# A new order of all steps, with the state products of batches 2 to 7 in blocks of three slices

## The chip, the cores and the metric

The kernel runs on one core of a Trainium2 chip. The metric is the time of one execution on the device in microseconds (us), as a median of several runs. The engines are PE (matrix products; PEld is its loading of weights), DVE, ACT and POOL (elementwise work), and SP, which here only issues transfers. Each engine works through its own queue in order, and waits on semaphores for the others. Sixteen DMA engines move data; they are fed by the queues of SP, ACT and POOL.

## The reference

Two stages in a row. The first lets 512 tokens and 32 state rows per batch and head attend to each other; the second is a feed-forward layer with the snake function.

```python
B, H, S, Ns, D = (8, 8, 512, 32, 64)      # x: (B,H,S,D), state: (B,H,Ns,D)
a = softmax(scale * x @ state.T)          # over the 32 state rows
xread = a @ state
a2 = softmax(scale * state @ x.T)         # over the 512 tokens
sread = a2 @ x
attn = concatenate([xread, sread], axis=2)            # (B, H, 544, D)
x2 = attn.transpose(0, 2, 1, 3).reshape(8 * 544, 512)
h = x2 @ w_in                             # 512 -> 2048
s = sin(alpha * h)
g = h + s * s / (alpha + 1e-9)
out = g @ w_out                           # 2048 -> 512, float32
```

Both softmaxes come from one table of exponentials, since the scores of the second are the transposed scores of the first.

## The kernel before

The whole program is one list of steps in a text, `ORDER` (line 21 on). A step such as `sq.0.2.V` calls the method `sq` of the class `Steps` with (0, 2, "V"). The order of the text is the order in each engine's queue; steps of different engines overlap as the semaphores allow. A last letter A, V or G gives the engine (ACT, DVE, POOL); a number where a bank is meant is one of the eight PSUM banks (`k.ps`, line 194). Each bank is a pool with one buffer: a new tile in a bank waits until every reader of the tile before it is done.

The unit of the work is a batch b (0 to 7) of 512 tokens; t = 8 is the group of all 256 state rows.

- **Loads.** POOL issues, with conversion to bf16, `l_st` (state, line 265), `lx` (x of batches 1 to 7, line 271), `li` (w_in in four quarters, line 280) and `lo` (w_out in four quarters, line 292). SP issues `l_s01` (state of batches 0 and 1) and `lq` (x of batch 0). `xnat` has three buffers.
- **Attention of a batch.** `pk` (DVE, line 344) sorts the tokens into `xp`, `td` (SP, line 387) transposes xp by DMA into `xT`; for batch 1 it is done on PE with `xt` (line 371) and copies `xc`, for batch 0 with `xtq`. `sc` (line 394) makes the scores on PE, `ex` the exponentials on ACT (which needs another table than Sin; a change of table is an ACT_TABLE_LOAD), `rs` and `rr` the sums and reciprocals on DVE, `nm` (line 418) the normalized table A, `ad` (SP, line 438) its transpose AT by DMA; in batch 0 `at` and `ac` do that on PE. `w` and `cs` (lines 445, 456) make the state side, `rc` and `xs` finish it on DVE.
- **State products.** Instead of xread @ w_in the kernel multiplies the state with w_in: `m` (line 478) makes one or two slices of M = state @ w_in of a batch, 512 columns of the 2048 each, on tiles of 64 rows by 32 columns; a slice is 8 matmuls and fills two banks (g = 0, 1). `me` (line 495) copies each bank to `M` in bf16. Slice s serves the feature blocks f = 4s to 4s+3. `st_t` and `st_c` transpose the state of batches 2 to 7 first, `s01_t` and `s01_k` that of batches 0 and 1.
- **Feed-forward.** For each f of 16: `h` (two matmuls of M with AT, line 531; `hg` is one of the two, line 549), `si` (Sin on ACT), `sq` (square on ACT, DVE or POOL, line 564), `gt` (s2 / alpha + h on DVE, line 573), which gives gT, the weights of the last product. For each quarter st of a batch, `o` (line 581) adds 16 matmuls gT x w_out in one bank; `oc` copies the bank to `o_sb` (six buffers), `os` (SP, line 597) writes it out. For t = 8, `h` has four matmuls of 256 columns. The last tile of all, (7, 3), is made in two pieces of 384 and 128 columns: `oh`, `och`, `osh`.
- **Warm-up.** `warm_up.n.cols.bank` (line 300) are matmuls without use in the first 17 us.

In the text before, `m` of batches 2 to 7 is called twelve times for two slices (four banks) each; `o.t.st.f0.f1` runs f0 to f1 in a row and every tile goes through f in rising order; `M` has two buffers, so the products of batch b + 2 can start only when the last `h` of batch b is done.

## Time and profile before

| | |
|---|---|
| time, median of 3 runs | 221.43 us (221.27 to 221.89) |
| the profiled execution | 221.22 us |
| its span, first to last instruction | 219.2 us |
| granted TensorE clock | 1.00 |
| ACT Sin, x144 | 88.8 us busy, mean 670 ns |
| DVE gt, x144 | 96.8 us busy, mean 713 ns |
| squares on POOL x75, ACT x53, DVE x16 | mean 1022, 594, 439 ns |
| copies of M: ACT x35, DVE x29 | mean 594, 679 ns |
| table loads for Exp and Sin on ACT | 5 and 5, 1283 ns each |
| transposes by DMA, issue to landing | AT 3.3 us, xT 4.8 us (medians) |
| output of one o tile (256 KB), issue to landing | 2.3 us (median) |

The busy time of an engine is the time in which it ran instructions. Matmuls are pipelined: the mean duration of one (373 to 379 ns for 512 columns) is longer than the distance from one to the next, which is read from a group of them in the chain of waits. An entry "A <- B: total, times, longest" of the waits says that A stood idle until B was done. Windows and timelines are in us from the start of the span.

### The profile page before, as it was taken

What the parts mean: (1) busy time and instruction counts of PE and PEld (TensorE: products, weight loads), DVE (VectorE), ACT (ScalarE), POOL (GpSimd) and SP (SyncE); (2) the same over time, 40 slices, a digit from 0 to 9 for tenths busy, and PEclk for the clock granted to TensorE, in tenths of its full rate; (3) what the DMA queues carried; (4) which work ended last, traced back from release to release, by engine and by line L of the source; (5) the groups of instructions that cost most, each with busy time, mean ns of one, the idle gap of its engine ahead of it and who ended that gap; (6) DMA issues with size and microseconds to landing.
All of it is one profiled execution on the core that took longest, in us unless ns stands there. A gap on an engine that the chain in (4) does not pass through costs nothing.

```text
span 219.2 us, 4303 instructions
## 1 busy us (share of the span) xinstructions
PE 211.4 (96%) x1593; PEld 104.5 (48%) x1619; DVE 162.9 (74%) x287; ACT 173.4 (79%) x297; POOL 106.2 (48%) x114
## 2 busy tenths in 40 slices
PE   7989999999999999999999999999999999999994
PEld 3744544444444534444454444454445555665452
DVE  3769996999787789989888788888667987661201
ACT  4799778997998979898996999798848896785111
POOL 5959533895195647753943387273501082121000
PEclk9999999999999999999999999999999999999999
DMA  6999999987491029167145327470220211012042
GB/s 195 178 206 204 205 204 146 217 169 133 101 238 48 3 92 143 57 144 96 48 79 131 109 71 96 134 110 0 48 100 0 98 48 48 0 51 96 1 143 96
DMA packets 38052, 23.48 MB, mean 107 GB/s; under 512 B 20992, under 2 KB 33680, under 8 KB 38032
## 3 DMA queue, kind: packets, MB, share of 16 engines
q1 hardware_dynamic: 26128, 15.08, 26.5%
q0 software_dynamic: 11648, 8.13, 26.0%
q8 instruction: 12, 0.20, 0.3%
q14 instruction: 8, 0.07, 0.1%
q10 hardware_dynamic: 256, 0.01, 0.1%
HBM read 17.44 MB, written 8.91 MB: 120 GB/s over the span
## 4 chain that ended last, share of the span: by engine, by line
PE 90%; DMA 6%; POOL 1%; issue 1%; ACT 0%
PE o_ps L587 54%; PE h_ps L537 22%; DMA w_in_sb<-in_moe_w_in_dram 5%; PE m_ps L488 4%; PE h_ps L543 3%; PE h_ps L552 2%; PE w_ps L450 2%; PE s_ps L399 2%; PE w_ps L461 1%; DMA s<-in_state_dram 1%; POOL w_in_sb L282 1%; PE x_ps L376 0%; POOL st_nat L267 0%; POOL s01b L255 0%; ACT o_sb L595 0%
## 5 line engine op out<-in xcount | busy, mean ns | idle before, releaser
L587 PE MATMUL o_ps<-w_out_sb,gT 128*128 128x512 bf16 (+2 forms) x542 | 133.9, 373 | 1.6 <-issue 1.0
L576 DVE SCALAR_TENSOR_TENSOR gT<-s,inva_sb,h_ps 128x512 bf16<-128x512 bf16 (+1 forms) x144 | 96.8, 713 | 20.4 <-POOL s L201 10.8
L201 POOL TENSOR_TENSOR s<-s 128x512 bf16<-128x512 bf16 (+1 forms) x75 | 75.9, 1022 | 64.4 <-ACT s L560 62.7
L560 ACT ACTIVATE s<-h_ps,alpha_sb 128x512 bf16<-128x512 f32 (+1 forms) x144 | 88.8, 670 | 11.1 <-PE h_ps L543 4.5
L587 PEld LDWEIGHTS <-gT 128*128 128x128 bf16 x560 | 52.3, 98 | 60.3 <-issue 5.0
L537 PE MATMUL h_ps<-AT,M 128*128 128x512 bf16 x219 | 60.0, 379 | 0.3
L537 PEld LDWEIGHTS <-M 128*128 128x128 bf16 x224 | 21.7, 98 | 25.9 <-issue 0.4
L569 ACT ACTIVATE s<-s 128x512 bf16<-128x512 bf16 (+1 forms) x53 | 31.4, 594 | 0.8
L201 POOL TENSOR_TENSOR A<-E,rR 128x512 bf16<-128x512 bf16 x16 | 16.6, 1056 | 23.8 <-ACT o_sb L595 12.9
L595 ACT COPY o_sb<-o_ps 128x512 f32<-128x512 f32 (+2 forms) x24 | 13.7, 570 | 16.6 <-PE o_ps L587 16.5
L496 ACT CAST M<-m_ps 128x512 bf16<-128x512 f32 x35 | 18.6, 594 | 8.2 <-PE m_ps L488 8.2
L496 DVE CAST M<-m_ps 128x512 bf16<-128x512 f32 x29 | 18.9, 679 | 2.5 <-PE m_ps L488 2.1
L595 DVE COPY o_sb<-o_ps 128x512 f32<-128x512 f32 x11 | 7.5, 685 | 12.9 <-PE o_ps L587 12.9
L201 DVE TENSOR_TENSOR s<-s 128x512 bf16<-128x512 bf16 (+1 forms) x16 | 7.0, 439 | 6.2 <-ACT s L560 6.1
L410 DVE TENSOR_REDUCE R<-E 128x16 f32<-128x512 bf16 x16 | 10.4, 657 | 0.7 <-ACT E L406 0.6
L488 PE MATMUL m_ps<-w_in_sb,stT 64*32 64x512 bf16 x256 | 10.2, 382 | 0.1
L468 DVE RECIPROCAL rC<-w_ps 128x128 f32<-128x128 f32 x8 | 7.6, 948 | 3.3 <-PE w_ps L461 3.2
L303 PE MATMUL warm_ps<-warm 128*128 128x128 bf16 (+3 forms) x66 | 8.6, 271 | 1.4 <-DVE warm L209 1.2
L552 PE MATMUL h_ps<-AT,M 128*128 128x512 bf16 x29 | 8.4, 379 | 0.9 <-ACT M L496 0.7
L406 ACT ACTIVATE E<-s_ps 128x512 bf16<-128x512 f32 x16 | 8.8, 602 | 0.4 <-PE s_ps L399 0.4
L543 PE MATMUL h_ps<-xs_all,w_in_sb 128*128 128x256 bf16 x64 | 9.1, 273 | 0.0
L543 PEld LDWEIGHTS <-w_in_sb 128*128 128x128 bf16 x64 | 6.3, 98 | 3.4
(56 smaller groups left out, 101.8 us busy)
## 6 DMA issues: line engine op xcount, KB each, us to landing
out_dram<-o_sb SPq DMA_DIRECT2D x33, 256.0 KB, 2.3
xnat<-in_x_dram POOLq DMA_DIRECT2D x7, 512.0 KB, 7.5
w_in_sb<-in_moe_w_in_dram POOLq DMA_DIRECT2D x4, 512.0 KB, 10.9
w_out_sb<-in_moe_w_out_dram POOLq DMA_DIRECT2D x4, 512.0 KB, 18.0
x<-in_x_dram SPq DMA_DIRECT2D x4, 256.0 KB, 4.2
st_nat<-in_state_dram POOLq DMA_DIRECT2D x1, 256.0 KB, 5.3
out_dram<-o_sb SPq DMA_DIRECT2D x1, 192.0 KB, 1.9
s<-in_state_dram SPq DMA_DIRECT2D x1, 128.0 KB, 2.2
```

Source lines behind the costliest of these rows:

```text
L201: {"V": k.nc.vector, "G": k.nc.gpsimd}[eng].tensor_tensor(out, a, b, ALU.mult)
L410: k.nc.vector.reduce_sum(R[:, g], k.t["E", b][:, g].rearrange("p c (h j) -> p (c h) j", j=k.Ns), axis=AX.X)
L488: k.nc.tensor.matmul(k.t["m", b, s + n, g][o0:o0 + k.Ns, :], k.stT[k.half(r), b * k.G + g, c0:c0 + k.Ns], k.w_in_sb[k.half(r), 2 * g + h, ...
L496: k.copy(eng)(k.t["M", b][:, g, s * k.FW:(s + 1) * k.FW], k.t["m", b, s, g][:])
L537: k.nc.tensor.matmul(hp[:, :n], k.t["M", t][:, g, fs], k.t["AT", t][:, g, :], start=(g == 0), stop=(g == k.G - 1),)
L543: k.nc.tensor.matmul(hp[:, :n], k.w_in_sb[:, q, fs], k.xs_all[:, q].rearrange("p b j -> p (b j)"), start=(q == 0), stop=(q == k.Q - 1),)
L552: k.nc.tensor.matmul(k.t["h", t, f][:], k.t["M", t][:, g, f * k.P:(f + 1) * k.P], k.t["AT", t][:, g, :], start=(g == 0), stop=(g == k.G - 1),)
L560: k.nc.scalar.activation(s[:, :n], k.t["h", t, f][:, :n], ACT.Sin, scale=k.alpha_sb[:, f:f + 1])
L569: k.nc.scalar.activation(s2[:, :n], s[:, :n], ACT.Square)
L576: k.nc.vector.scalar_tensor_tensor(gT[:, :n], k.t["s2", t, f][:, :n], k.inva_sb[:, f:f + 1], k.t["h", t, f][:, :n], ALU.mult, ALU.add,)
L587: k.nc.tensor.matmul(k.t["o", t, st, half][:, cols], k.t["gT", t, f][:, rows], k.w_out_sb[:, f, cols], start=(f == 0), stop=(f == k.FT - 1),)
L595: k.copy(eng)(o_sb[:, cols], k.t["o", t, st, half][:, cols])
```

## The change

The list of steps is replaced as a whole. Each step still does what it did, with these differences in the functions: `M` gets a third buffer; `xt` transposes both heads of a pair at once from `xp` (it read `xnat` one head at a time), so that it now stands behind `pk`; `hg` may take its two halves, and `o` its 16 feature blocks, in any order, with the bank taken by steps of their own (`ho`, `oo`) and the first and last matmul found by counting (`made`).

```diff
-        k.mpool, k.epool, k.smallp = pool("mpool", 2), pool("epool", 4), pool("smallp", 4)
+        k.mpool, k.epool, k.smallp = pool("mpool", 3), pool("epool", 4), pool("smallp", 4)
...
-                for r in range(2):
-                    k.nc.tensor.transpose(
-                        tp[k.half(r), h, i * k.P:(i + 1) * k.P],
-                        k.t["xnat", b][:, 2 * (2 * g + h) + r, i * k.D:(i + 1) * k.D],
-                        k.ident[:],
-                    )
+                k.nc.tensor.transpose(
+                    tp[:, h, i * k.P:(i + 1) * k.P], k.pair(b, i, 2 * g + h), k.ident[:]
+                )
...
+    def ho(k, t, f, bank):
+        k.t["h", t, f] = k.ps(bank, [k.P, k.S], FP32, "h_ps")
+        k.made["h", t, f] = 0
...
-            start=(g == 0), stop=(g == k.G - 1),
+            start=k.made["h", t, f] == 1, stop=k.made["h", t, f] == k.G,
...
+    def oo(k, t, st, bank, half=None):
+        k.t["o", t, st, half] = k.ps(bank, [k.P, k.DOUT], FP32, "o_ps")
+        k.made["o", t, st, half] = 0
+
+    def o(k, t, st, f, half=None):
...
+        k.made["o", t, st, half] += 1
+        k.nc.tensor.matmul(
+            k.t["o", t, st, half][:, cols], k.t["gT", t, f][:, rows], k.w_out_sb[:, f, cols],
+            start=k.made["o", t, st, half] == 1, stop=k.made["o", t, st, half] == k.FT,
+        )
```

Of the list, the parts of which the prediction speaks. The head:

```diff
-zero.1 identf.V lq.3.S s01_c.G l_st li.0 xq.0.A s01_t.4 li.1 xtq.0.5 warm_up.1.384.3 xq.1.A
-s01_k.1.V s01_k.0.A li.2 xtq.1.6 warm_up.2.448.3 xc.0.0.0.V xq.2.A xc.0.0.1.V lo.0 al_t.7 xq.3.A
...
+touch_x l_s01 consts touch lq.0.S ident_ l_alpha lq.1.S zero.0 warm_up.8.512.7 exp_table lq.2.S
+zero.1 identf.V lq.3.S s01_c.G li.0 xq.1.A warm_up.1.256.7 s01_t.0 warm_up.1.512.7 xtq.1.1 xq.0.A
+xtq.0.2 xq.2.V xtq.2.3 s01_k.0.A xq.3.V xtq.3.4 xc.0.0.1.A li.1 xc.0.0.0.A s01_k.1.V sc.0.0.0 ex.0.0
+xc.0.1.1.V xc.0.1.0.V warm_up.2.512.7 sc.0.1.3 ex.0.1 rs.0.0 rr.0.0 ho.0.5.4 al_t.2 rs.0.1
+warm_up.5.512.7 m.0.0.3.0 li.2 sin_table lx.1.0.1 rr.0.1 m.1.0.1.5 nm.0.0.0.4.G warm_up.1.512.7
+at.0.0.6 me.0.0.0.A me.0.0.1.A nm.0.1.0.4.V at.0.1.7 ac.0.1.A ho.0.2.3 ac.0.0.V me.1.0.0.V hg.0.2.0
+ho.0.1.0 hg.0.1.0 hg.0.2.1 al_c inva m.0.1.2.1 me.0.1.0.V me.1.0.1.A l_st ho.0.4.5 m.1.1.7.6
+me.1.1.1.V me.1.1.0.V lo.0 si.0.2 lo.1 me.0.1.1.A hg.0.1.1 hg.0.4.1 si.0.1 hg.0.4.0 si.0.4 sq.0.2.G
+gt.0.2 sq.0.4.V sq.0.1.G hg.0.5.1 gt.0.1 hg.0.5.0 si.0.5 ho.0.0.6 sq.0.5.G warm_up.1.512.2 m.0.2.7.1
+me.0.2.1.A hg.0.0.1 me.0.2.0.A hg.0.0.0 gt.0.4 ho.0.6.3 hg.0.6.0 si.0.0 sq.0.0.G hg.0.6.1 ho.0.3.1
+hg.0.3.1 m.1.2.2.0 me.1.2.0.A me.1.2.1.A ho.0.7.7 hg.0.7.0 hg.0.3.0 hg.0.7.1 gt.0.5 li.3 ho.0.11.5
+pk.1.1.V hg.0.11.1 ho.0.10.2 si.0.3 hg.0.10.0 hg.0.11.0 si.0.11 pk.1.0.V xt.1.1.0 gt.0.0 xc.1.1.1.V
+sq.0.3.G xt.1.0.4 xc.1.0.0.A xc.1.1.0.V si.0.7 xc.1.0.1.V hg.0.10.1 st_t.1.6 st_c.1.1.A gt.0.3
+st_c.1.0.A st_t.0.0 ho.0.9.4 st_c.0.0.A hg.0.9.1 st_c.0.1.V hg.0.9.0 ho.0.8.1 hg.0.8.0 hg.0.8.1
+sq.0.11.G gt.0.11 si.0.6 sc.1.1.6 oo.0.0.0 o.0.0.2 si.0.9 o.0.0.3 oo.0.2.5 o.0.2.3 sq.0.6.G sq.0.7.V
+o.0.2.1 o.0.2.2 gt.0.7 o.0.2.0 o.0.0.1 sq.0.9.V lo.2 gt.0.6 o.0.0.0 oo.0.3.7 o.0.3.1 o.0.3.3 o.0.3.2
+si.0.10 o.0.3.0 si.0.8 oo.0.1.3 o.0.1.6 gt.0.9 o.0.1.1 o.0.1.7 o.0.1.2 o.0.1.4 o.0.2.4 o.0.1.0
...
+o.0.0.5 o.0.3.6 m.0.3.6.4 me.0.3.0.A m.1.3.1.2 me.1.3.1.V o.0.1.3 nm.1.0.0.4.G o.0.3.5 o.0.3.4
...
+o.0.1.11 sq.0.12.V o.0.2.10 lx.2.0.1 si.0.13 o.0.1.10 gt.0.12 o.0.3.11 o.0.2.9 o.0.1.8 o.0.3.15
+lx.4.0.1 gt.0.14 sq.0.13.A o.0.0.9 o.0.0.4 lx.3.0.1 h.1.12.1 si.1.12 h.1.3.6 si.1.3 gt.0.13 h.1.5.4
```

The state products of batches 2 to 7, of which the first two pairs and the first two blocks, and the group around batches 5 and 6:

```diff
-rs.2.0 o.1.1.10.11 m.2.2.2.4.3.0 rr.2.0 rs.2.1 o.1.2.13.14 nm.2.0.0.4.G me.2.3.0.A o.1.2.14.15 w.0.1
...
-m.2.0.3.4.0.2 ad.2 rc.0 o.1.3.7.8 me.2.1.1.A o.1.3.8.9 sc.3.0.7 xs.0.1 me.2.1.0.A o.1.1.11.12 os.1.2
...
+w.0.6 cs.0 nm.2.1.0.4.G m.2.3.0.3 m.2.2.7.1 m.2.0.4.5 me.2.0.1.A o.1.2.13 o.1.2.4 me.2.0.0.A
...
+sc.3.1.3 ex.3.1 rs.3.1 o.1.3.5 o.1.0.3 o.1.3.11 o.1.3.4 m.2.1.3.6 m.3.1.2.1 m.3.0.7.0 me.2.1.0.A
...
+m.5.0.7.3 m.5.1.1.2 me.5.3.1.V me.5.3.0.V me.5.1.1.V oc.3.0.A o.3.2.6 td.6 oo.4.3.0 o.4.3.9
...
+rs.5.1 rr.5.1 o.3.2.0 o.3.2.10 o.3.2.15 o.3.2.2 rr.5.0 oc.3.2.A os.3.2 m.5.2.1.2 m.6.2.7.6 m.6.1.3.4
...
+pk.7.0.V ex.6.0 rs.6.0 rr.6.0 o.4.3.0 me.5.2.0.A m.6.0.1.4 m.6.3.2.5 m.7.2.3.7 me.7.2.0.A me.7.2.1.V
```

The tail:

```diff
-o.7.0.8.9 oc.8.1.A o.7.0.9.10 oc.8.0.V o.7.0.10.12 os.8.1 o.7.0.12.13 os.8.0 o.7.0.13.16 o.7.2.0.2.2
-oc.7.0.A o.7.2.2.5 os.7.0 o.7.2.5.11 oh.7.3.0.1 o.7.2.11.13 och.7.3.0.A o.7.2.13.15 osh.7.3.0
-o.7.2.15.16 oh.7.3.1.4 oc.7.2.V os.7.2 och.7.3.1.A osh.7.3.1
...
+sq.8.13.G o.7.2.10 oh.7.3.0.5 o.8.0.2 gt.8.13 o.8.0.13 o.7.1.13 oc.7.1.V o.8.1.11 o.8.0.3 os.6.1
+o.8.0.6 oc.8.0.V os.8.0 o.8.1.7 o.8.1.13 och.7.3.0.V osh.7.3.0 oc.7.0.V os.7.1 o.7.2.0 os.7.0
+o.7.2.12 o.8.1.1 oc.8.1.A os.8.1 o.7.2.8 o.7.2.1 oc.7.2.V oh.7.3.1.5 os.7.2 och.7.3.1.A osh.7.3.1
```

Counted over the list: squares on ACT 53 before and 32 after, on DVE 16 and 47, on POOL 75 and 65; `nm` on POOL 16 and 11, on DVE 0 and 5; `me` on ACT 35 and 37, on DVE 29 and 27; output copies on ACT 24 and 27, on DVE 11 and 8; warm-up matmuls 66 and 19; table loads the same.

## Prediction

> **What bounds the kernel now.** I read the page's busy shares first, then the waits of PE, then the chain of waits, then timelines of three places: the head, one block of state products, the tail.
>
> ```profile
> PE 211.4 (96%) x1593; PEld 104.5 (48%) x1619; DVE 162.9 (74%) x287; ACT 173.4 (79%) x297; POOL 106.2 (48%) x114
> ...
> PE h_ps L552 <- ACT M L496: 0.7, 1, 0.7
> ...
> 5.58 11.79 DMA w_in_sb<-in_moe_w_in_dram
> 17.37 0.04 issue
> 17.41 0.62 PE m_ps L488 x16
> ```
>
> The chain is PE nearly all the way from 17.41 us, where PE had waited for the third quarter of w_in; after that the waits view has no wait of PE that matters. So three things can move the time: when unbroken PE work starts, how much of it there is, and what follows the last matmul. From 17.41 to the end of the last matmul (216.13 in the chain) are 198.7 us. The rows give the same: 248 h matmuls and 528 o of 512 columns, 776 x 0.216 (29 in 6.26 us in the chain) = 167.6; the cut last o tile 3.5; 64 of h.8 x 0.109 = 7.0; 28 slices of m x 0.216 = 6.0; sc, w, cs and xt 9.9; sum 194.0. The rest is changes of matrix shape:
>
> ```profile
> 50.81 2.54 PE L587 MATMUL o_ps<-w_out_sb,gT 128*128 128x512 bf16 x11
> 53.28 0.63 PE L488 MATMUL m_ps<-w_in_sb,stT 64*32 64x512 bf16 x16
> 53.84 0.61 PE L587 MATMUL o_ps<-w_out_sb,gT 128*128 128x512 bf16 x2
> ```
>
> Eleven o should take 2.37, m starts after 2.47: 0.10 lost going in. Sixteen m matmuls are two passes of 0.216 (eight run side by side), the next o starts after 0.56: 0.13 lost coming out. So a run of another shape costs about 0.22; the order has 23 such runs (m, xt, cs), two of them touching: 4.9. Sum 198.9 against 198.7: PE is full here, and nothing is left to win except those 4.9 us, the head and the tail.
>
> **PE work of the new order.** It has, from its m.0.2 on: 776 x 0.216 = 167.6, 3.5, 7.0, 28 slices 6.0, sc, w and cs 8.8, xt as 16 full transposes of 0.056 (four in 0.23) 0.9, st_t 32 x 0.034 = 1.1; sum 194.9. Runs of another shape: m.0.2, m.1.2, st_t, m.0.3 with m.1.3, the eight episodes, five of cs: 17 x 0.22 = 3.7. Together 198.6, less the 0.2 by which the count was high before: 198.4. So the episodes and the joined runs save 1.2, and st_t, which moves into this stretch, gives back most of it. The o as single steps in any order are the same 528 matmuls; the third buffer of M is room alone, since each M takes the place of one whose last h is long done: nothing for either.
>
> **Start.** q0, the queue of POOL's loads, moves 1.14 MB from 11.8 to 17.4 us (views of the DMA by window), 0.204 MB/us, 512 KB in 2.55 us, in the order of issue. Before, li.2 lands at 5.58 + 11.79 = 17.37 behind st_nat (256 KB). With l_st moved behind lx.1, li.2 lands 1.25 earlier, 16.1; lx.1 18.7, l_st 19.9, lo.0 one load later than before (19.9 + 2.55 = 22.45), lo.1 25.0; li.3 has the same loads ahead as before, so 27.6, lo.2 30.1, lo.3 32.7. With m.0.2 at 16.15 and no wait the last matmul would end at 16.15 + 198.4 = 214.5, **1.6 earlier**. The loads allow it: by the rows PE reaches the first o (lo.0) at 22.9, o.0.1.6 (lo.1) at 25.5, m.0.3 (li.3) at 28.1, o.0.0.8 (lo.2) at 30.9, o.0.3.15 (lo.3) at 34.4, each 0.5 to 1.7 after its load. The engines allow it less. ACT's queue from me.1.0.1 (done about 13.75: sin_table ends at 11.6, then four copies) to si.0.3 has six Sin (0.69 alone, 0.58 in a row) and five copies (0.54): 6.6, so si.0.3 ends at 20.3; sq.0.3 on POOL 1.04; gt.0.3 stands behind three xc copies on DVE and ends at 22.8. hg.0.8 needs its bank; PE would be there at 22.2. **0.6 lost**, and 0.2 more at m.1.3, whose bank waits for gt.0.8 (29.0).
>
> lx.2 is now issued by POOL behind sq.0.14, at about 34, not at 15.2. Such a load lands 5.6 to 7.3 after its issue once the queue is empty, 39.7 to 41.4; pk.2.1 stands in DVE's queue at about 40.1 with gt.1.6 and gt.1.0 behind it, and h.1.2 and h.1.7 wait for their banks: 0 to 1.3, I take 0.2. SP issues td.2, td.3 and td.4 ahead of the first outputs; os.0.1 goes out at about 64 behind td.4 and lands 2.3 later, and oc.1.1, which needs its buffer (six of o_sb), comes near 75: nothing, as long as ad.3 and td.4 are on time. Of 66 warm-up matmuls 19 stay: the longest pause of PE before (0.73 at 13.05) left the granted clock at 1.00, the new pauses are up to 0.6: nothing.
>
> **Episodes.** Three slices hold six banks, so six tiles must be evacuated ahead and six after. Before m.2.3 the rows give ex.2.0 and gt.1.4 done where PE arrives, within 0.1; afterwards PE has o for 0.9 us before it needs the first bank, whose copy ends at 0.7. The same sums at m.5.3 to m.6.0 (nine slices in 11 us) leave 0.1 of wait. I take nothing here, up to 0.1 an episode in the range.
>
> The Trainium skill (TensorEngine Tiling, PSUM Bottleneck) says that packing speeds up PE and not the evacuation, which can become the bottleneck: it speaks against this change. By it each episode would cost 6 x 0.6 on two engines less its own 0.87, 0.9, in all 7.4, time about 230; the rows of the pair at 53.28 show four copies and no wait of PE behind them.
>
> **Who computes the squares.** Counting steps: squares on ACT 53 to 32, on DVE 16 to 47, on POOL 75 to 65; nm on DVE 0 to 5. ACT loses 21 x 0.594 = 12.5 and gains some 3.5 of copies; POOL loses 10 x 1.02 + 5 x 1.06 = 15.5; DVE gains 31 x 0.439 = 13.6 and the five nm, which no row shows on DVE: between the square's 0.42 and gt's 0.75; I take 0.6, nearer to gt for its third operand, 3.0; it loses about 3 of copies. DVE ends at 176. In the densest part, m.0.3 to m.3.2, its rows sum to 46.2 in 46.8 us of PE work (42.6 where gt, in a row, take 0.66); before, m.1.3 to m.3.0, 40.8 in 47.2. And these squares have a second price:
>
> ```profile
> 38.37 0.42 DVE L201 TENSOR_TENSOR s<-s 128x512 bf16<-128x512 bf16 x1 [0.28 <-ACT s L560]
> 43.12 0.58 DVE L201 TENSOR_TENSOR s<-s 128x512 bf16<-128x512 bf16 x1
> ...
> 41.38 2.04 POOL L201 TENSOR_TENSOR s<-s 128x512 bf16<-128x512 bf16 x2 [0.19 <-ACT s L560]
> ```
>
> Of the 16 DVE squares 13 of full width ran beside an idle POOL and took 0.42. The two that met a POOL square took the rest of it and 0.28 more: 43.12 to 43.42, end at 43.70; likewise 61.62 (0.66). With 52 such operations and POOL busy 82 of 219 us, a meeting costs up to 0.9, on average 0.38, so 52 x 0.375 x 0.38 = 7.4 if they fall at random, nothing if they all fall in POOL's pauses. DVE's room in the dense parts is about 4 us in 47, and what DVE is late, banks and gT are late. I take 0.6 on PE's path, bounds 0 and 5.
>
> **Tail.** Before, PE ends at 216.13 and the span 3.07 later:
>
> ```profile
> 214.68 2.10 SPq L602 DMA_DIRECT2D out_dram<-o_sb  x3
> 215.26 0.69 DVE L595 COPY o_sb<-o_ps 128x512 f32<-128x512 f32 x1 [7.09 <-PE o_ps L587]
> 216.15 0.27 ACT L595 COPY o_sb<-o_ps 128x128 f32<-128x128 f32 x1 [1.50 <-PE o_ps L587]
> ...
> L602 SPq DMA_DIRECT2D out_dram<-o_sb x33: 332/333/949, 40.9 to 216.4; - x33
> ...
> L605 SPq DMA_DIRECT2D out_dram<-o_sb x2: 609/692/775, 207.9 to 208.8; - x2
> ```
>
> In the new order oc.7.1 waits on DVE for o.7.1.13, after the first oh.7.3, and oc.8.0, och.7.3.0, oc.7.0 and oc.7.2 queue behind it, though o.7.0 is done before. From the end of that oh, DVE's copies end at 1.5, 2.2, 2.7, 3.4, 4.1; PE ends at 3.9. SP then issues os.8.0 (2.24), osh.7.3.0, os.7.1, os.7.0, os.8.1, os.7.2 and at 5.0 the last, which was ready at 4.2: 0.75 late. These are 1.53 MB; writes run at up to 0.38 MB/us (the tail's view of the DMA), so from 3.0 they land at 7.1, 3.2 after PE's end, where before the last landed 1.9 after it. Between +0.75 and +1.3; I take **+1.1**.
>
> **Sum.** PE's end 216.13 - 1.6 + 0.8 + 0.2 + 0.6 = 216.1; the tail 3.07 + 1.1 = 4.2: span 220.3. The profiled run took 221.22 with 219.2 of span, 2.0 more; the median 221.43 is 0.2 above it. So 220.3 + 2.2 = **222.5**, +0.5%.
>
> **Rivals.** (1) Faster: the earlier head carries through. Its place is the queue of loads (li.2 1.25 earlier), its price -1.6 at the last matmul; it decides as long as what PE waits for later and what the tail adds stay under 0.9 together. With the tail at its lower bound and no wait that is 221.43 - 1.6 + 0.75 = 220.6. For it: no wait in the steady part of the old trace, at 0.87 of DVE load. Against: the head's 0.6, which is a plain sum of ACT's queue. Chance 0.28, most of it over 0.3%. (2) DVE becomes the bound: meetings with POOL cost 5 us or more on DVE beyond its room. It decides from about 4 us in the stretch 34 to 62; PE's end about 220, time 226.5. For it: 0.98 of load by unpacked durations. Against: gt in a row are shorter. Chance 0.17. (3) The episodes do not shorten PE's work, because the loss belongs to each slice and not to each run: +0.9 on the sum, 223.4; against it singles and pairs lose the same 0.22 (28.18: 8 matmuls, 0.34). Inside the forecast's range; chance 0.05. Forecast: 0.5, its own range 221.4 to 224.3.
>
> The range reaches into (1) and (2): 220.4 to 226.5. A measurement of this kernel tells 0.3% from no change, 220.8 and 222.1: faster 0.22, within 0.18, slower 0.60.
>
> **What would show it.** m.0.2 at 16.1 and the first o near 23.5; m runs of 24 matmuls with 0.22 lost at each; DVE squares of 0.6 to 1.3 beside POOL squares; five outputs issued on SP within 3 us of the end and a tail over 3.8. I am wrong if PE ends before 215, if the tail stays at 3.1, or if PE's waits for DVE exceed 4 us.

## The result

| | before | changed |
|---|---|---|
| time, median of 5 runs | 221.27 us (220.98 to 221.89) | 233.55 us (232.95 to 233.79) |
| the profiled execution, its span | 221.22, 219.2 us | 233.72, 231.9 us |
| first matmul of m.0.2 | 17.41 us | 15.70 us |
| end of the last matmul | 216.13 us | 222.69 us |
| tail behind it | 3.07 us | 9.2 us |

The ratio is 1.0544, with an interval of 1.0522 to 1.0565: slower, as forecast, but by 12.3 us where 1.1 was forecast, and outside the range. The span is 12.7 us longer: 6.6 of that ahead of the end of the last matmul, 6.1 behind it. Both were terms of the forecast's sum, and neither had the right size.

The page of the changed kernel, its busy shares, PE and DVE in 40 slices, and the chain by engine:

```profile
PE 214.8 (93%) x1556; PEld 102.5 (44%) x1556; DVE 182.5 (79%) x319; ACT 166.5 (72%) x280; POOL 92.5 (40%) x99
...
PE   7889799979999999989999999999999999999940
...
DVE  2898998999999988799989898978896658744240
...
PE 61%; DVE 20%; ACT 5%; DMA 4%; issue 2%; POOL 2%; ACTq 0%; POOLq 0%; DVEq 0%
```

Before, the chain read:

```profile
PE 90%; DMA 6%; POOL 1%; issue 1%; ACT 0%
```

Now a fifth of it is DVE. The last slice of PE is empty and the one ahead of it 40% busy: that is the tail. The granted clock is 0.99 in the mean of the span, but the windows (busy time of PE, PEld, DVE, ACT and POOL, then the clock) show it at 1.00 until well behind the last matmul, so it took nothing from PE:

```profile
0.00:222.70 222.70, 214.80 (x1556) 102.50 (x1556) 182.50 (x319) 166.20 (x279) 92.47 (x99) 1.00 0.50 98
...
227.10:231.90 4.80, 0.00 (x0) 0.00 (x0) 0.00 (x0) 0.00 (x0) 0.00 (x0) 0.51 0.29 95
```

DVE has 19.6 us more to do than before (162.9). Why is seen in the groups of DVE by form (busy time, mean ns of one, idle time before):

```profile
L577 DVE SCALAR_TENSOR_TENSOR gT<-s,inva_sb,h_ps 128x512 bf16<-128x512 bf16 x128 | 91.0, 742 | 14.9 <-POOL s L202 8.6 <-ACT s L570 4.2
L202 DVE TENSOR_TENSOR s<-s 128x512 bf16<-128x512 bf16 x42 | 22.6, 541 | 4.5 <-ACT s L561 4.3
...
L349 DVE COPY xp<-xnat 128x1024 bf16<-128x1024 bf16 x14 | 8.7, 634 | 0.0
L202 DVE TENSOR_TENSOR A<-E,rR 128x512 bf16<-128x512 bf16 x5 | 4.1, 817 | 0.1
```

and, of the kernel before:

```profile
L201 DVE TENSOR_TENSOR s<-s 128x512 bf16<-128x512 bf16 x15 | 6.7, 449 | 6.2 <-ACT s L560 6.1
L348 DVE COPY xp<-xnat 128x1024 bf16<-128x1024 bf16 x14 | 5.5, 429 | 0.1
```

gT costs what it did (742 ns before, too). A square went from 449 to 541 ns in the mean, a packing copy (`pk`), which nobody touched, from 429 to 634. How one comes to be long is seen in the timeline of 47 to 51 us (start, duration; in brackets the idle time before, and who ended it):

```profile
46.66 4.39 POOL L202 TENSOR_TENSOR s<-s 128x512 bf16<-128x512 bf16 x4
...
47.79 2.37 DVE L349 COPY xp<-xnat 128x1024 bf16<-128x1024 bf16 x2
...
50.08 1.40 DVE L577 SCALAR_TENSOR_TENSOR gT<-s,inva_sb,h_ps 128x512 bf16<-128x512 bf16 x2
...
50.87 0.59 PE L535 MATMUL h_ps<-AT,M 128*128 128x512 bf16 x2 [1.49 <-DVE gT L577]
```

Two copies that take 0.75 together stand 2.37 us, beside four squares in a row on POOL; gT behind them is late, its bank of h comes free late, and PE idles 1.49 us. The tail is seen on SP's queue:

```profile
221.02 0.78 SPq L608 DMA_DIRECT2D out_dram<-o_sb  x1
221.91 2.06 SPq L605 DMA_DIRECT2D out_dram<-o_sb  x3
224.06 0.72 SPq L608 DMA_DIRECT2D out_dram<-o_sb  x1
224.88 1.34 SPq L605 DMA_DIRECT2D out_dram<-o_sb  x2
```

Seven sends, of which the two on line 608 are outputs of the state rows. The last is issued at 225.75, 3.1 us behind the last matmul (0.3 before), and lands 5.2 us later (1.8 before): together the 6.1 us.

To see where PE falls behind, I matched the loads of PE's weights, in their order, with the steps of the text, and counted the work done (o and each half of h 0.216 us, a slice of m 0.22, w, cs, h.8, 0.22 for a change of shape; the preparations of batches 0 and 1 and warm-ups not). The table gives the time in us at which a kernel has done so much; three experiments are in it that come below (skipmet: ten POOL squares left out; both: the end re-spaced besides; b_eng: the order before with the new engines).

```
work done   before   changed   skipmet    both    b_eng
     6       20.14     18.44     18.61    18.51    20.19
    20       35.88     37.71     37.01    36.84    37.28
    30       45.81     48.36     47.63    48.46    48.51
    35       51.24     55.70     53.97    54.65    54.52
    60       77.24     82.17     79.84    80.52    81.13
   100      117.88    123.71    120.99   121.19   125.39
   140      159.00    165.88    162.02   162.23   167.66
   195      213.98    221.18    217.33   217.54   222.65
```

The changed kernel leads by 1.7 us at work 6, is 1.8 behind at 20, 4.5 at 35, 5.8 at 100 and 7.2 at 195 (0.6 comes back in the last products, since it changes shape less often). So the loss is no single place: 3.5 us in the head, 2.6 from 38 to 56 us, the rest in pieces of 0.2 to 0.8.

### The profile page after: what moved, and what is told of

The parts are those of the page before. It is cut to its first block, busy times and chain, and to the rows that moved or that the text cites. A ratio compares the mean times of both kernels' runs of the same rounds, so it can differ in the third digit from the quotient of the medians.

```text
span 231.9 us, 4176 instructions
## 1 busy us (share of the span) xinstructions
PE 214.8 (93%) x1556; PEld 102.5 (44%) x1556; DVE 182.5 (79%) x319; ACT 166.5 (72%) x280; POOL 92.5 (40%) x99
## 4 chain that ended last, share of the span: by engine, by line
PE 61%; DVE 20%; ACT 5%; DMA 4%; issue 2%; POOL 2%; ACTq 0%; POOLq 0%; DVEq 0%
PE o_ps L590 38%; PE h_ps L535 12%; DVE gT L577 11%; DVE s L202 4%; ACT s L561 3%; PE m_ps L486 3%; DMA w_in_sb<-in_moe_w_in_dram 3%; PE h_ps L541 3%; DVE xp L349 2%; POOL s L202 2%; DVE M L494 2%; PE w_ps L448 2%; PE w_ps L459 1%; DMA s<-in_state_dram 1%; PE s_ps L397 1%
## 5 line engine op out<-in xcount | busy, mean ns | idle before, releaser
L590 PE MATMUL o_ps<-w_out_sb,gT 128*128 128x512 bf16 (+2 forms) x560 | 138.8, 373 | 2.3 <-DVE gT L577 1.5
L202 POOL TENSOR_TENSOR s<-s 128x512 bf16<-128x512 bf16 (+1 forms) x65 | 66.2, 1029 | 87.9 <-ACT s L561 75.5
L535 PE MATMUL h_ps<-AT,M 128*128 128x512 bf16 x224 | 62.4, 379 | 2.2 <-DVE gT L577 2.0
L202 DVE TENSOR_TENSOR s<-s 128x512 bf16<-128x512 bf16 (+1 forms) x47 | 24.6, 526 | 7.8 <-ACT s L561 7.6
L202 POOL TENSOR_TENSOR A<-E,rR 128x512 bf16<-128x512 bf16 x11 | 12.0, 1099 | 32.6 <-DVE rR L414 15.5
L598 ACT COPY o_sb<-o_ps 128x512 f32<-128x512 f32 (+1 forms) x27 | 15.5, 574 | 10.7 <-PE o_ps L590 10.6
L570 ACT ACTIVATE s<-s 128x512 bf16<-128x512 bf16 (+1 forms) x32 | 19.0, 596 | 0.7
L553 PE MATMUL h_ps<-AT,M 128*128 128x512 bf16 x32 | 9.2, 380 | 0.6 <-DVE AT L434 0.3
L349 DVE COPY xp<-xnat 128x1024 bf16<-128x1024 bf16 x14 | 8.7, 634 | 0.0
L598 DVE COPY o_sb<-o_ps 128x512 f32<-128x512 f32 (+1 forms) x8 | 5.1, 668 | 4.1 <-PE o_ps L590 4.1
L304 PE MATMUL warm_ps<-warm 128*128 128x512 bf16 (+1 forms) x19 | 7.0, 486 | 1.2 <-DVE warm L210 1.2
```

Of the source, the lines that this page charges most:

```text
L202: {"V": k.nc.vector, "G": k.nc.gpsimd}[eng].tensor_tensor(out, a, b, ALU.mult)
L349: k.copy(eng)(k.t["xp", b][:, :, hs, :], k.t["xnat", b][:, hs, :].rearrange("p h (i d) -> p i h d", i=k.C),)
L535: k.nc.tensor.matmul(hp[:, :n], k.t["M", t][:, g, fs], k.t["AT", t][:, g, :], start=(g == 0), stop=(g == k.G - 1),)
L570: k.nc.scalar.activation(s2[:, :n], s[:, :n], ACT.Square)
L590: k.nc.tensor.matmul(k.t["o", t, st, half][:, cols], k.t["gT", t, f][:, rows], k.w_out_sb[:, f, cols], start=k.made["o", t, st, half] == 1 ...
L598: k.copy(eng)(o_sb[:, cols], k.t["o", t, st, half][:, cols])
```

## The experiments: the tail

**The end re-spaced.** The changed kernel with another order of its last steps; the copy of 7.0 goes from DVE to ACT with it:

```diff
-o.7.1.2 o.7.1.12 o.7.0.0 o.8.0.0 ... oh.7.3.0.5 o.8.0.2 gt.8.13 o.8.0.13 o.7.1.13 oc.7.1.V ...
-och.7.3.0.V osh.7.3.0 oc.7.0.V os.7.1 o.7.2.0 os.7.0 o.7.2.12 o.8.1.1 oc.8.1.A os.8.1 ...
+o.7.0.0 oc.7.0.A os.7.0 o.7.1.2 o.7.1.12 o.7.1.13 oc.7.1.V os.6.1 os.7.1 o.8.0.0 ...
+o.8.0.13 oc.8.0.V os.8.0 o.8.1.7 o.8.1.13 o.8.1.1 oc.8.1.A os.8.1 oh.7.3.0.5 och.7.3.0.V ...
```

> The changed kernel with its last 33 steps in another order: output 7.0 is finished, copied and sent first, then 7.1, 8.0 and 8.1, each as soon as its last product is there, then the first part of 7.3, the last five products of 7.2, and the second part of 7.3 in a bank of its own. No work is added or taken away. Theory A (six outputs sent within three microseconds are what the last transfers wait for): the span after the last product falls from 9.2 to 3.1-3.8 us and the run to 227.5-228.5. Theory B (the tail is long because of something else, such as the size or the address of the last outputs): the tail stays above 7 us and the run above 231. What is lost ahead of the end (about 8.5 us of PE) stays in both.

228.49 us (228.36 to 228.61), 5.06 less than the changed kernel; ratio to the kernel before 1.0316 (1.0297 to 1.0336). The span is 226.3, with PE's end 0.1 later than in the changed kernel: 5.7 us are gone from the tail, which is 3.5 us now, as theory A said.

**The reverse, on the kernel before.** Four sends put behind the first part of 7.3, nothing else:

```diff
-... oc.7.1.A ... os.7.1 ... oc.8.0.V o.7.0.10.12 os.8.1 o.7.0.12.13 os.8.0 ... os.7.0 ... osh.7.3.0 ...
+... osh.7.3.0 os.7.1 os.8.1 os.8.0 os.7.0 o.7.2.15.16 oh.7.3.1.4 oc.7.2.V os.7.2 ...
```

> The kernel before with its last outputs held back: the sends of 7.1, 8.1, 8.0 and 7.0 stand behind the send of the first part of 7.3 on SP's queue, so seven sends (1.75 MB less a quarter) are issued in the last 1.5 us of the products and behind them. No engine's work is touched. Theory A (a bunch of outputs costs what the changed kernel's tail shows): the span after the last product rises from 3.1 to 8-9.5 us, the run to 226.5-228. Theory B (what the changed kernel's tail lost is the copies out of PSUM, not the transfers): within 1.5 us of 221.4.

225.78 us, 4.4 over the kernel before (221.40 beside it); ratio 1.0187 (1.0149 to 1.0226). Less than theory A said and far over theory B: the products end where they did (216.0), so the sends alone cost this.

Both runs moved the sends of the state rows with the others, and the sends one by one raise another suspicion (start of the send, in brackets its landing after so many us; S is an output of the state rows, whose landing the trace does not have; read from the trace):

```
before           S 207.87   S 208.76   209.82 (4.4)   214.68 (1.9)   215.98 (2.0)   216.44 (1.8)
changed          S 221.02   221.91 (4.2)   222.31 (4.2)   223.11 (4.0)   S 224.06   224.88 (5.9)   225.75 (5.2)
end re-spaced    215.81 (2.0) 216.24 (2.4) 216.71 (2.6) S 218.29 S 219.18 221.40 (3.0) 222.67 (2.4) 223.12 (2.2)
held back        214.60 (1.9) 214.98 (2.2) S 215.46 S 216.34 217.00 (4.8) 217.81 (4.6) 219.17 (3.4)
```

What stands behind an S within 2 us lands after 4.2 to 5.9 us, what stands 2 to 3 us behind one after 3.0 to 4.0, what stands elsewhere in these tails after 1.8 to 2.6, even in threes. So the bunch may be innocent.

**The state rows alone moved.** The changed kernel with the products, copies and sends of 8.0 and 8.1 some 4 us earlier. The other five sends stay in a bunch at the end, behind the row of copies on DVE; the copy of 8.0 goes to ACT, so that this row is one copy shorter:

```diff
-o.7.1.2 o.7.1.12 o.7.0.0 ... oh.7.3.0.5 ... oc.8.0.V os.8.0 ... oc.8.1.A os.8.1 ... oc.7.2.V ...
+o.8.0.13 oc.8.0.A os.6.1 os.8.0 o.8.1.13 oc.8.1.A os.8.1 o.7.0.0 o.7.2.10 oh.7.3.0.5 ...
```

> The changed kernel with the two outputs of the state rows (8.0, 8.1) finished, copied and sent some 4 us before the last matmul; the other five sends stay bunched at the end, behind the same late copies on DVE. In the re-spaced end both things were changed at once. Theory A (a bunch of sends is what the tail costs, whatever they are): five sends are left in it, the tail stays at 7 us or more and the run above 231. Theory B (the transfers of the state rows take some 5 us to clear, and whatever is sent just behind them lands late: in the kernel before a tile sent 1.1 us behind them landed after 4.4 us instead of 1.9, in the changed kernel 5.9 and 5.3): the last landing falls from 5.3 to 2-3 us, the tail to 4-5.5 and the run to 228.5-230.

229.63 us (229.41 to 229.76), 3.9 less than the changed kernel; ratio 1.0381 (1.0362 to 1.0399). SP's queue, and the transfers of 214 to 228 us in 40 slices:

```profile
218.17 1.49 SPq L608 DMA_DIRECT2D out_dram<-o_sb  x2
222.21 2.51 SPq L605 DMA_DIRECT2D out_dram<-o_sb  x5
```

```profile
DMA  0000000000000000643445455599999998100000
GB/s 0 0 0 0 0 0 0 0 0 0 0 0 0 0 0 29 76 35 47 146 176 217 176 205 193 199 373 394 386 375 404 369 392 272 32 0 0 0 0 0
```

Five sends (three of 256 KB, one of 192, one of 64) in 2.5 us now land after 2.0 to 2.8 each, at 370 to 400 GB/s. The state rows, in the first half of the busy slices, have the transfer engines 0.3 to 0.6 busy and move 29 to 217; sent from 218.2 us on, they move from 219.3 to about 223.1. So theory B holds, as far as the landing goes. The tail is 4.2 us (PE ends at 223.3 here), 5.0 less than in the changed kernel, in two parts. The last output lands 2.5 us after its send instead of 5.2; and it is sent 0.8 us behind the last matmul instead of 3.1. That second part is not the copies: in the changed kernel all of them were done by 223.0 us, and the last send left at 225.75. SP itself was late there: the three tile sends behind the first state rows took it 2.06 us to issue, 0.69 each, where five take 2.51 here, 0.50 each, and the second send of state rows (0.72) stood among them.

Moving the state rows is thus worth 3.9 of the 5.1 us that the re-spaced end won; the other 1.2 are not taken apart. The run held back on the kernel before moved the state rows too, so it does not speak for the bunch. Why these transfers are slow no run here tells.

## The experiments: DVE beside POOL

**The meeting by itself.** A kernel of its own with the tile sizes of this one:

```diff
+for f, n, pools in ((act_meet, 1, 1), (sq_alone, 8, 0), (sq_alone, 0, 8), (sq_meet, 14, 8), (pk_alone, 8, 0),
+                    (pk_meet, 14, 8), (gt_meet, 10, 8), (rs_meet, 12, 8), (me_meet, 10, 8), (act_meet, 12, 8)):
+    meet()          # all engines wait for one another
+    pool(pools)     # so many squares on POOL
+    for i in range(n): f(i)
```

> A measurement by itself; the computation of the kernel is left out, and the output is one tile of ones. On the kernel's own tile sizes: squares on DVE alone, squares on POOL alone, then POOL squares beside each of: DVE squares, packing copies of DVE, the DVE operation that makes gT (one input in PSUM), the DVE sum, the DVE copy out of PSUM, and ScalarE squares. Theory A (a lock between DVE and POOL): squares of 0.42 and copies of 0.36-0.42 us rise to about 1.0 and more each while POOL squares run, since each waits for a whole square of POOL of about 1.04; the gT operation (0.74), the copy out of PSUM (0.68) and the ScalarE square (0.60) stay within 0.03 of what they are alone. Theory B (a shared bandwidth): all DVE operations that read SBUF rise, the gT operation too, by some 10 to 40 per cent.

Its groups by form: line 515 is POOL's square, 518 and 521 the DVE square alone and beside POOL, 524 and 527 the copy alone and beside POOL, 530 the gT operation, 533 the sum, 536 the copy out of PSUM, 539 the square on ACT, the last four beside POOL.

```profile
L515 POOL TENSOR_TENSOR gouta<-gsrc 128x512 bf16<-128x512 bf16 x29 | 31.6, 1089 | 0.0
...
L533 DVE TENSOR_REDUCE red<-src 128x16 f32<-128x512 bf16 x12 | 8.2, 685 | 0.4
L527 DVE COPY douta<-wide 128x1024 bf16<-128x1024 bf16 x7 | 6.3, 897 | 0.0
...
L521 DVE TENSOR_TENSOR douta<-src 128x512 bf16<-128x512 bf16 x7 | 6.3, 896 | 0.0
...
L539 ACT ACTIVATE douta<-src 128x512 bf16<-128x512 bf16 x7 | 4.3, 616 | 0.0
...
L530 DVE SCALAR_TENSOR_TENSOR douta<-src,one,hp 128x512 bf16<-128x512 bf16 x5 | 3.7, 733 | 0.0
...
L536 DVE CAST douta<-hp 128x512 bf16<-128x512 f32 x5 | 3.4, 682 | 0.0
...
L518 DVE TENSOR_TENSOR douta<-src 128x512 bf16<-128x512 bf16 x4 | 1.7, 420 | 0.0
...
L524 DVE COPY douta<-wide 128x1024 bf16<-128x1024 bf16 x4 | 1.6, 412 | 0.0
```

The means of 521 and 527 hold pairs that ran before and after POOL's eight; its timeline shows what one meeting is:

```profile
18.92 1.23 POOL L515 TENSOR_TENSOR gouta<-gsrc 128x512 bf16<-128x512 bf16 x1
...
19.17 1.26 DVE L521 TENSOR_TENSOR douta<-src 128x512 bf16<-128x512 bf16 x1
20.11 1.22 POOL L515 TENSOR_TENSOR goutb<-gsrc 128x512 bf16<-128x512 bf16 x1
20.36 1.25 DVE L521 TENSOR_TENSOR doutb<-src 128x512 bf16<-128x512 bf16 x1
```

The two take turns: the DVE square waits for the rest of POOL's (1.26 instead of 0.42, so 0.84 lost), and POOL's next waits for it (1.22 instead of 1.04, 0.18 lost). Packing copies do the same. gT, the sum, the copy out of PSUM and ACT's square were not run alone here; beside POOL they take 733, 685, 682 and 616 ns, within 0.03 us of their means in the changed kernel (742, 667, 678, 596), where POOL is idle 60% of the time. So theory A holds. The Trainium skill (SBUF — State Buffer, Who interferes with whom) says just this: DVE and GpSimd share one pair of ports as a lock that one instruction holds to its end; a copy in a fast mode takes it, and so does an operation with two inputs in SBUF against a GpSimd operation that reads SBUF, while one with at most one input in SBUF and no such mode does not. These rows agree with it in every form tried here.

**Everything that was lengthened, moved away from DVE.**

```diff
-pk.1.1.V sq.0.7.V sq.0.9.V nm.1.1.0.4.V pk.2.1.V pk.2.0.V sq.1.15.V pk.3.1.V pk.3.0.V ...
+pk.1.1.A sq.0.7.A sq.0.9.A nm.1.1.0.4.G pk.2.1.A pk.2.0.A sq.1.15.A pk.3.1.A pk.3.0.A ...
```

> The changed kernel with the DVE operations that were lengthened beside a POOL square on other engines: 11 squares of DVE and 6 packing copies on ScalarE, 2 normalisations on POOL; the order is not touched. Theory A (a DVE operation with two SBUF inputs, or a fast copy, waits while POOL squares, and PE waits for what is late behind it): some 9.8 us of DVE's lengthening goes, PE's lost time between 15.7 and 222.7 falls from 8.5 to 2-4 us, the run to 227.5-229.5. Theory B (PE loses its time to the order itself, to the head or to loads that come late): less than 2 us are won, 231.5-233.5. Theory C (ScalarE becomes the bound by the work put on it): slower than 233.

236.38 us (235.93 to 238.32), 2.8 slower than the changed kernel. DVE did get rid of it (full-width squares 444 ns in the mean, busy 170.1 us), but ACT, at 176.8, had 7.44 us of work in the 7.47 from 42.4 to 49.9, and PE waited for output copies on ACT (1.8 and 1.6 us in the two longest entries of its waits) as well as for gT (2.3). Theory C; the run says nothing on the first two.

**Only the squares, to ACT.** The same without the copies and normalisations:

```diff
-sq.0.7.V sq.0.9.V sq.1.15.V sq.2.13.V sq.2.0.V sq.3.7.V sq.4.3.V sq.5.7.V sq.6.7.V sq.6.1.V sq.8.1.V
+sq.0.7.A sq.0.9.A sq.1.15.A sq.2.13.A sq.2.0.A sq.3.7.A sq.4.3.A sq.5.7.A sq.6.7.A sq.6.1.A sq.8.1.A
```

> The changed kernel with the 11 lengthened squares of DVE on ScalarE and nothing else; the packing copies and normalisations stay on DVE, unlike in the run in which all of them were moved (236.4 us). Theory A (there, the packing copies of about 1 us each and the squares of stretch 42 to 58 filled ScalarE; elsewhere the squares' move helps): 232-233.5. Theory B (ScalarE is as full as DVE all along): 234.5-236.5.

233.22 us (232.68 to 233.75): theory A's side, but only 0.3 better than the changed kernel. So the six copies on ACT and the two normalisations on POOL were what made the run before it slower.

**POOL's side, to ACT.** The ten POOL squares that lay under lengthened DVE operations:

```diff
-sq.0.6.G sq.0.10.G sq.1.1.G sq.1.9.G sq.2.7.G sq.2.9.G sq.4.13.G sq.4.11.G sq.5.12.G sq.6.6.G
+sq.0.6.A sq.0.10.A sq.1.1.A sq.1.9.A sq.2.7.A sq.2.9.A sq.4.13.A sq.4.11.A sq.5.12.A sq.6.6.A
```

> The changed kernel with ten POOL squares that lay under lengthened DVE operations (0.6, 0.10, 1.1, 1.9, 2.7, 2.9, 4.11, 4.13, 5.12, 6.6) on ScalarE; DVE keeps all 47 squares and every copy. Theory A (the lock is what PE waits for in the end): DVE's squares of full width fall from 541 to about 470 ns in the mean, its packing copies from 634 to about 480, and the run by 2.5-4 us to 229.5-231. Theory B (DVE's load): DVE's busy time falls, but PE's lost time by less than 1 us: 232.5-233.5. Theory C (ScalarE has no room for 10 x 0.63 us either): 233.5-235, with PE's waits behind ScalarE.

233.00 us (232.22 to 233.68), 0.55 better. DVE's squares fell to 471 ns, its copies to 474, as theory A has it, but the time is in theory B's range, 2 us above theory A's. PE's waits for gT fell from 3.5 to 1.6 us in all; those for output copies on ACT, 0.3 before, rose to 1.4, with ACT 4.7 us busier.

**Two of them alone**, 1.1 and 1.9, those beside the copies at 47.8:

> The changed kernel with two of the ten squares that POOL runs without a pause from 39.9 to 51.1 us (1.1 and 1.9, at 47.7 and 48.7) on ScalarE; no operation of DVE is changed. Theory A (the lock): the two packing copies of batch 3 stood 2.37 us on DVE beside these squares and come down to 0.8-1.2 us together, PE's wait of 1.66 us at 50.9 falls to under 0.6, and the run is 1.0-1.8 us faster: 231.7-232.6. Theory B (it is DVE's load, not the company of POOL): the copies stay at 2.2-2.4 us and the run at 233.2-234.

233.71 us (232.43 to 234.38): no gain, which is theory B's figure. The timeline of 47 to 52 us, from the fastest of the four runs, shows theory A's signs all the same, and where the gain went:

```profile
47.86 0.75 DVE L349 COPY xp<-xnat 128x1024 bf16<-128x1024 bf16 x2
...
49.32 0.59 PE L535 MATMUL h_ps<-AT,M 128*128 128x512 bf16 x2
...
50.23 0.39 PE L397 MATMUL s_ps<-stT,xT 128*128 128x64 bf16 x8 [0.32 <-ACT o_sb L598]
...
51.30 0.39 PE L397 MATMUL s_ps<-stT,xT 128*128 128x64 bf16 x8 [0.46 <-ACT o_sb L598]
```

The two copies came down from 2.37 to 0.75 us though DVE's own work was not touched, and PE's wait of 1.49 for gT is gone: the lock made them long. But the next scores now wait for output copies, which stand on ACT behind the two squares it was given. The wait went from DVE to ACT, at least in part. Up to here the lock was shown and not its price, since each cure paid on ACT.

**The ten left out, against ten others left out.** In both, `gt` uses the sine where the square is missing, so no engine gets work:

```diff
+        if eng == "N":
+            k.t["s2", t, f] = k.t["s", t, f]
+            return
```

> The changed kernel without ten of POOL's 65 full-width squares, those under lengthened DVE operations (0.6, 0.10, 1.1, 1.9, 2.7, 2.9, 4.11, 4.13, 5.12, 6.6); gT is made from the sine itself there. No work is put on another engine. With the same ten on ScalarE the run was 233.0 us. Theory A (the meeting of DVE and POOL is what PE's lost time comes from; on ScalarE the work was paid again): 229.5-231. Theory B (the meetings are covered by something else): 232.5-233.5.

> The control: the changed kernel without ten other POOL squares near to those but beside no lengthened DVE operation (0.3, 0.11, 1.4, 1.5, 2.4, 2.6, 3.8, 3.9, 5.10, 6.3). As many waits of gT for POOL fall away as in the run without the ten that meet. Theory A (the meeting): 232.8-233.6, at least 1.5 us behind the other. Theory B (what counts is that ten squares less are to be done at all): both within 0.6 us of each other.

229.89 us (229.21 to 230.16) and 233.73 us (233.27 to 234.22). Ten squares less on POOL are worth nothing; the ten that meet are worth 3.7. DVE's groups and PE's waits for gT, first without the ten that meet:

```profile
L202 DVE TENSOR_TENSOR s<-s 128x512 bf16<-128x512 bf16 x42 | 19.0, 455 | 3.7 <-ACT s L561 3.6
L349 DVE COPY xp<-xnat 128x1024 bf16<-128x1024 bf16 x14 | 6.4, 470 | 1.5 <-DMA xnat<-in_x_dram 1.5
...
PE h_ps L535 <- DVE gT L580: 0.7, 2, 0.5
...
PE o_ps L593 <- DVE gT L580: 0.2, 1, 0.2
```

and without the ten others:

```profile
L202 DVE TENSOR_TENSOR s<-s 128x512 bf16<-128x512 bf16 x42 | 22.2, 532 | 4.5 <-ACT s L561 4.3
...
L349 DVE COPY xp<-xnat 128x1024 bf16<-128x1024 bf16 x14 | 8.9, 650 | 0.3 <-DMA xnat<-in_x_dram 0.3
...
PE h_ps L535 <- DVE gT L580: 2.4, 4, 1.5
PE o_ps L593 <- DVE gT L580: 1.5, 3, 0.7
```

Against the changed kernel DVE is rid of 5.9 us in the first (3.6 on the squares, 2.3 on the copies), and the end of PE's products moves from 222.7 to 218.8: two thirds of what these ten cost DVE reaches PE. The meetings that stay (squares at 455 ns against 420 alone, copies at 470 against 412) are not in the 3.7.

**Order against engines.** The engines of all squares and normalisations exchanged between the two orders; in `b_eng` the order is that before, 98 of 160 engine letters differ:

> The kernel before, in its own order, with the engines of the changed kernel for all 144 squares and 16 normalisations: DVE has 47 squares and 5 normalisations instead of 16 and none, ScalarE 32 squares instead of 53, POOL 65 instead of 75. Nothing else of the change. Theory A (the squares' move to DVE, beside POOL, makes PE late whatever the order): 227-231. Theory B (it is the new order that is late): 221.4-223.5.

> The other half of the square of four: the changed kernel's order with the engines of the kernel before for all squares and normalisations. Theory A (the squares on DVE are the cause): 229-231, so 2.5-4.5 us better than the changed kernel, its tail (9.2 us) still there. Theory B (the order is late by itself): 233-236, no better. Theory C (each assignment fits its own order only): both mixed kernels are slower than the kernel that their order comes from.

230.53 us (229.65 to 230.70), 9.2 over the kernel before, and 258.07 us, 24.5 over the changed kernel. So 31 squares more on DVE make even the old order late, with the same lengthening; DVE's groups and PE's waits (us in total, times, longest):

```profile
L201 DVE TENSOR_TENSOR s<-s 128x512 bf16<-128x512 bf16 x42 | 22.7, 540 | 3.3 <-ACT s L560 2.9
L348 DVE COPY xp<-xnat 128x1024 bf16<-128x1024 bf16 x14 | 7.7, 584 | 0.0
```

```profile
PE h_ps L537 <- DVE gT L576: 2.4, 4, 0.9
PE o_ps L587 <- DVE gT L576: 1.4, 4, 0.8
```

But the other mixture is far worse, which theory C says and theory A does not: each list of engines fits its own order alone. Part of its 24.5 us is the clock: PE stood still for 3.9 us up to 144.8, and from 142.9 to 153.1 us its granted clock was 0.50, so that, as an estimate, up to 5 us (half of these 10.2) are no price of the squares at all. And 98 letters differ in either mixture, not only the 31 squares. The 9.2 us are thus no measure of the squares' move within the change.

## The experiments: the rest

**Both causes away.** The end re-spaced, and the ten that meet left out.

> The changed kernel with the re-spaced end and without the ten POOL squares that meet (gT from the sine there): the two causes taken away at once. If they are separate, their gains add: 233.55 - 5.06 - 3.66 = 224.8, so 224.3-225.5 us, and some 3.5 us over the kernel before are left for other causes. If they overlap (products that end earlier find the transfers as late as before), 226 or more.

224.01 us (223.50 to 225.44), ratio 1.0133 (1.0090 to 1.0175): the two add, with 0.8 us to spare. They make 9.5 of the 12.3; 2.6 us over the kernel before (221.44 beside it) are left. By the table of work done they arise before 55 us, and then no more.

**The head.** On top of that, the load and the transposes of the other states where the kernel before has them:

```diff
-s01_c.G li.0 ... st_t.1.6 st_c.1.1.A ... st_c.1.0.A st_t.0.0 ... st_c.0.0.A hg.0.9.1 st_c.0.1.V
+s01_c.G l_st li.0 ... rs.0.1 st_t.0.6 st_c.0.0.A st_c.0.1.V st_t.1.5 st_c.1.1.A st_c.1.0.A
```

> As the run with both causes taken away, and besides the load of the other states stands ahead of the first weights again, and their 32 transposes and 4 copies stand ahead of the first slice m, as in the kernel before. Theory A (the weights' early arrival was bought with about 1 us of transposes and 0.7 us of waits for stT in the stretch where PE could have been full): the first weights land 1.0-1.3 us later, but PE has done the same work at 37 us 0.3-1.0 us earlier, and the run is 0.3-1.0 us faster. Theory B (early weights pass through to the end): 0.8-1.3 us slower.

224.80 us (224.67 to 225.15), 0.8 slower in the median, at the lower end of theory B; the runs of the two overlap (223.50 to 225.44), so what is sure is that going back gains nothing. The transposes can be seen: from work 6 to work 20 PE took 17.3 us, against 18.3 without this edit and 15.7 in the kernel before. But work 6 came 1.5 later, and 0.5 of that was left at work 20. How much of the new head's lead is real these profiles do not tell: the third quarter of w_in landed 0.97 later here (16.61 us against 15.64), and with one and the same head it landed anywhere from 14.93 (without the ten that meet) to 16.44 (without the ten others).

**The loads of x.** Also on top of both: x of batch 2 issued at 22.7 instead of 35.0 us, its packing copies at 36 to 37.

```diff
-lo.2 gt.0.6 ... lx.2.0.1 si.0.13 ... lx.4.0.1 gt.0.14 ... lx.3.0.1 ... pk.2.1.V ... pk.2.0.V
+lo.2 lx.2.0.1 gt.0.6 ... gt.0.12 pk.2.1.V ... lx.3.0.1 lx.4.0.1 gt.0.14 pk.2.0.V
```

> As the run with both causes taken away (224.0 us), and besides the loads of x stand earlier on POOL's queue: batch 2 behind the third quarter of w_out, at about 24 instead of 35 us, batch 3 ahead of batch 4; the two packing copies of batch 2 follow at about 37-38 us, in POOL's pause, instead of 41 to 43. Theory A (the late loads push four packing copies into the stretch from 41 to 50, where DVE is full, and that is most of what is left): PE's lag behind the kernel before at the work that this has done by 51 us falls from 3.4 to about 2, the run by 0.8-1.5 us to 222.5-223.3. Theory B (the rest is spread over the order): 223.6-224.5. Against A: the earlier load may delay the last quarter of w_out, which the products of slices 12 to 15 need.

224.41 us: theory B. The copies took 0.42 each in POOL's pause, as meant, and two DVE squares behind them now met POOL instead (1.21 and 1.27 us at 39.1 and 43.2). The last quarter of w_out landed at 35.14 instead of 32.78 us, and PE did not wait for it. So the last 2.6 us are not settled: they lie in the stretch to 55 us, where DVE has no room, and moved about in it with each mend.

**Mended with all work kept:** the end, the loads, two squares on ACT.

> The changed kernel with all of its work, mended as far as these runs allow: the re-spaced end, the loads of x earlier as above, and two of POOL's squares (1.1, 1.9) on ScalarE. Gains of 5.1 (end), 0.5-1.5 (loads) and 0-0.5 (squares) from 233.55: 226.5-228, still over the kernel before, since the meetings elsewhere stay.

228.81 us, outside the expected 226.5 to 228 and no better than the end alone. What was said against the earlier load came true here: the last quarter of w_out, issued behind it, landed at 37.90 us (34.00 in the changed kernel), and PE stood 1.0 us for it. No version here beats the kernel before.

**The episodes broken up**, twice: first with o products from ahead of each episode put between its slices, then with products from behind it.

```diff
-m.2.3.0.3 m.2.2.7.1 m.2.0.4.5 ... o.1.2.13 o.1.2.4
+m.2.3.0.3 o.1.2.13 m.2.2.7.1 o.1.2.4 m.2.0.4.5
```

> The changed kernel with its eight episodes broken up: between the three slices of each stand the last two o products that stood ahead of it, so 8 runs of the other matrix shape become 24. Theory A (each run costs about 0.22 us, as taken in the prediction): 16 runs more are 16 x 0.22 = 3.5 us on a full PE, and somewhat less where PE waits anyway: the run at 235.5-237.5. Theory B (the loss is by slice, not by run): no change, 233.2-234. So this measures what the episodes by themselves give.

> The eight episodes broken up again, but with o products that stood behind each episode moved up between its slices, so that no slice comes earlier than in the changed kernel; in the first try products from ahead of it were used, and each first slice came two products earlier and waited for its bank. Theory A (a run of the other shape costs 0.22 us on a full PE): 16 x 0.22 = 3.5 us, the run at 236.5-237.5. Theory B (the first try's 0.39 us for a run is the price itself): 239-240.5.

239.89 and 239.62 us: 6.3 and 6.1 over the changed kernel for 16 more runs of m, not 3.5. The first is outside both ranges, the second in theory B's, by its figure 0.39 for a run. Yet the timeline shows no more than 0.23 for a run, here in the second try:

```profile
124.54 0.41 PE L487 MATMUL m_ps<-w_in_sb,stT 64*32 64x512 bf16 x8
124.88 0.39 PE L591 MATMUL o_ps<-w_out_sb,gT 128*128 128x512 bf16 x1
125.20 0.41 PE L487 MATMUL m_ps<-w_in_sb,stT 64*32 64x512 bf16 x8
```

From one slice to the next, with one o between, are 0.66 us; slice and o are 0.216 each, so 0.23 for the change of shape both ways, as the forecast took it. Wherever one o stands between two slices, in either try, the distance is the same 0.66. 16 x 0.23 = 3.7; the other 2.4 us are not explained. The rival by slices is out, and a run costs at least what the forecast took; nothing in these runs speaks against the episodes as such.

## Why the prediction was wrong

**Right.** The direction, and the terms on PE: m.0.2 at 15.70 (forecast 16.1), first o at 23.56 (23.5), runs of 24 matmuls with 0.22 lost each, no wait of PE behind an episode. The time of the first o is in part luck: the wait of 0.6 that was put at hg.0.8 did not come there, and 0.58 came at the first o itself, whose bank the copy of the transposed states on DVE still read. The sum by which the bottleneck of evacuation would make the episodes cost 7.4 us did not come true: the copies of M kept their 0.60 and 0.68, and at all eight episodes the next product started 0.77 us after the first of the 24 matmuls. The clock stayed at 1.00 with 19 warm-up matmuls, as said. DVE squares of 0.6 to 1.3 beside POOL, and a bunch of sends at the end, were named as what to look for; both are there.

**Wrong, the tail.** The step that failed: "Between +0.75 and +1.3; I take **+1.1**". It is +6.1 in the profiles. The forecast had the order of the sends right, the state rows among the last, and gave all of them one rate, 1.53 MB at 0.38 MB/us. The state rows do not move at that rate, and what stands behind them is issued and lands later. The profile before had shown it: of its last four tiles the one sent 1.1 us behind the state rows landed after 4.4 us, the other three after 1.8 to 2.0. (A smaller slip: the last output before landed 1.84 us after its issue, but 2.15 after PE's end, from which the forecast counts; its own sum so gives +1.05.)

**Wrong, the meetings.** The step: "I take 0.6 on PE's path, bounds 0 and 5." Shown is 3.7 for ten POOL squares alone. That is inside the bounds, and far from the choice; what the other meetings cost PE is not measured. Two errors are in it. The 52 operations counted were squares and normalisations; the 14 packing copies were left out, though by the measurement they are lengthened alike (0.41 to 1.26), and they lost 2.9 us (14 x (634 - 429) ns). And DVE was given about 4 us of room in 47: in the stretch from 42.9 to 55.7 it had none, busy 5.50 of 5.50 and 7.31 of 7.34 us, so what a meeting took there could not be made up on DVE. The rate itself was about right: the forecast's 0.375 x 0.38 for 52 operations and 14 copies would be 9.4 us on DVE, and full-width squares, copies and normalisations lost about 9 (42 x 0.12 = 5.0, 2.9, and 5 x 0.19 over the shortest of 0.63 = 0.9). What was wrong is how much of it DVE could hide. PE's waits for DVE are 5.0 us by the waits view (3.5 of them for gT), over the 4 that were named as a sign of being wrong.

**Wrong in part, the head.** Forecast: 1.6 won, 1.0 lost to waits. Of the lead of 1.7 at work 6 the kernel is 1.8 behind at work 20, a loss of 3.5; with the ten meetings away 1.1 behind (from a lead of 1.5), a loss of 2.7. So waits and the states' transposes took 2.7 there, where the forecast had 1.0 of waits and 1.1 for these transposes inside PE's work. The load of batch 2, taken as 0.2, made its copy wait 0.23 us in the run with both causes away, but brought it next to a POOL square (1.28 us); there PE loses 1.5 from work 25 to 30.

**The rivals.** The second, DVE as the bound, came true in part: in its place (34 to 62 us) the kernel lost 2.6 us from 38 to 56, but 3.5 had gone ahead of that, and PE's end, put at 220, was 222.7; the tail came on top. It was given 0.17 since DVE's average left room. The first had its lead and lost it; the third is out.
